# A greedy issue planner replaced by a fixed issue table, with MLP1 sums regrouped and the modulation rows sent through DRAM

## Chip, cores and metric

The kernel runs on one core of a Trainium2 chip. The metric is the device time of one execution in microseconds (us). The kernel before has a median of 216.2 us over 5 runs (215.92 to 216.38).

## Reference

One adaLN block with S = 2048 tokens and D = 512 channels, all bfloat16. `c` gives six modulation rows; a local dilated attention (window 8, step 2, 32 heads of 16) and a token-mixing MLP (2048 to 1792 to 2048, over tokens, not channels) follow.

```python
mod = (silu(c) @ w_mod).reshape(1, 6, 1, -1)        # sa, ca, ga, sb, cb, gb
h = layernorm(x) * (1 + ca) + sa
x = x + ga * attention(h, wqkv, wo)                 # k, v of positions s, s-2, ..., s-14
h = layernorm(x) * (1 + cb) + sb
hn = layernorm(h)                                   # the MLP's own norm
u = gelu(einsum('bsd,sf->bdf', hn, w1) + b1)        # sum over tokens s
y = einsum('bdf,fs->bds', u, w2) + b2
x = x + gb * y.transpose(0, 2, 1)
```

MLP1 sums over tokens, so no unit of it is complete before the last token tile has been through attention.

## The kernel before

**Tiles and chunks.** The tokens are 16 tiles of 128 (`st` = 0 to 15), taken through attention in five chunks of 2, 4, 4, 4 and 2 tiles (`SIZES`). MLP1's 1792 outputs are 14 units of 128 (`ft`), MLP2's tokens again 16 tiles.

**Steps and names.** Every piece of work is an `_Op` with a name, an engine (or a choice of two), what it reads and writes, and at times a buffer of a pool that it takes or frees. For a chunk `c` the steps are: `ln1s` (DVE statistics of x), `rstd1`/`nb1` (ACT and DVE, a tile's scale and shift), `n1` (the norm itself, on ACT, DVE or POOL as the strings `NE` say), `tr` and `hT` (transposes on PE and their copies; chunks 2 to 4 use DMA transposes `xt`), `wsc` (scaling of the qkv weights by 1+ca), `qkv` and `ev` (projection and copy out of PSUM), `vd` (16 DMAs a chunk that lay out shifted v), `qk` (DVE products q*k, 128x4096), `red` (PE sums of them over 16 channels), `max`, `sub`, `exp`, `esum`, `rcp`, `smB` (softmax), `a2` (weights spread to partitions), `pv` (DVE products, 128x4096) and `pvacc` (PE sums), `oev`, `wo` (output projection, residual), `x1` (copy to x), `ln2s` or `ln2q`/`ln2m` (second norm's statistics, on DVE or on ACT), `n2`, `aff` (times 1+cb, plus sb, on DVE), `ln3s`, `rstd3`, `h3` (the MLP's norm). `red`, `pvacc`, `a2` use 32-column tiles of the PE array (four matmuls side by side); all other matmuls use the whole array.

**MLP.** MLP1 is done in three levels over token tiles 0-5, 6-9 and 10-15 (`BOUNDS=(6, 10)`) for all 14 units. After level 0 the sums are parked in `gT` as bfloat16 (`park0`); level 1 begins with a matmul that puts them back into PSUM (`inj1`, `INJ=(1,)`) and parks again (`park1`); level 2 gets them added by DVE (`padd2`), then `gelu` on ACT. MLP2 is one group of 14 matmuls a tile (`mlp2`), then two DVE operations (`fin`) and a store.

**Modulation rows.** `build_mod_rows` forms ga, sb, 1+cb and gb as rows spread over all 128 partitions: `sc_rep` (silu(c) repeated over 128 columns) is the stationary operand, four matmuls of 512 columns a row, and ACT copies each row out of PSUM. `woq_s` multiplies the output weights by ga.

**Order.** `G.schedule()` simulates the engines at build time with a duration for each op, and at each step issues the op that can start first, with ties inside a window of 0.02 us (`WIN`) broken by the ranks `RANK`; `BIAS` shifts work between ACT and DVE. Each engine then runs its list in that order and waits in order. All compute instructions are recorded through one helper, so the profile shows them as line 238; tiles tell them apart. All DMAs but one are issued by SP; each waits for the one eight places before it.

**Warm-up.** 36 small matmuls (`warm`) and 42 planned ones (`filler`) run on PE before its first real work.

Of the kernel before, what the change touches and what calls it, by code (L numbers as in the profile page):

```python
# [8 lines left out]
ALU = mybir.AluOpType  # L9
# [14 lines left out]
class _Op:  # L24
    __slots__ = ("idx", "alts", "eng", "dur", "lat", "fn", "name", "deps", "succ", "start", "end", "bytes_", "pk", "bias",
                 "alloc", "frees", "behind", "locks", "desc")

    def __init__(self, idx, alts, lat, name, bytes_, pk):
        self.idx, self.alts, self.lat, self.name, self.bytes_, self.pk = idx, alts, lat, name, bytes_, pk
        self.eng, self.dur, self.fn = alts[0]  # L30
        self.deps, self.succ = set(), []
        self.start = self.end = None
# [9 lines left out]
class _Graph:  # L42
    XLAT = 0.05
    OVERLAP = {"dve": 0.08, "act": 0.1}
    PE_DRAIN = 0.17
    LANES = 8
    RING = 132
    PWAIT = 3.0
    WIN = 0.25

    def __init__(self, pools):
        self.pools = pools
        self.ops = []
        self.last_writer = {}
        self.readers = {}
        self.pk = 0.0
# [4 lines left out]
    def add_any(self, alts, reads=(), writes=(), name="", lat=0.0, after=(), bytes_=0, pk=None, bias=0.0, alloc=None,  # L61
                frees=None, behind=None, locks=False, desc=0):
        op = _Op(len(self.ops), list(alts), lat, name, bytes_, self.pk if pk is None else pk)
        op.bias, op.alloc, op.frees, op.behind = bias, alloc, frees, behind
        op.locks, op.desc = locks, desc
# [27 lines left out]
    def filler(self, t, n, k):  # L93
        f = _Op(-1, [("pe", n * 0.06, lambda: self.fill_fn(k, n))], 0.0, "filler", 0, 0.0)
        f.start, f.end = t, t + n * 0.06
        f.alloc = f.frees = f.behind = None
        f.locks, f.desc = False, 0
        return f

    def schedule(self):  # L100
        ops = self.ops
        for o in ops:
            for d in o.deps:
                ops[d].succ.append(o.idx)
        eng_free = {}
        dmaq = []
        locked = []

        def pool_end(r, d):
            t = r  # L110
            for a, b in locked:
                if b <= t:
                    continue
                if a > t:
                    if a - t >= d:
                        return t + d
                    d -= a - t
                t = b
            return t + d + (self.PWAIT if len(locked) > 4 else 0.0)
        ndeps = {o.idx: len(o.deps) for o in ops}  # L120
        avail = set(o.idx for o in ops if not o.deps)
        free = {k: {i: 0.0 for i in range(n)} for k, n in self.pools.items()}
        order = []

        def pick(slot):
            f = free[slot.pool]
            if slot.size == 1:
                return min(((f[k], (k ^ 1) in f, k) for k in f), default=None)
            return min(((max(f[k], f[k + 1]), k) for k in f if k % 2 == 0 and k + 1 in f), default=None)

        dep_ready = {}

        def ready_time(o, e):
            r = dep_ready.get((o.idx, e))
            if r is None:
                r = 0.0
                for d in o.deps:
                    od = ops[d]
                    if od is o.behind or od.eng == e == "pe":
                        t = od.start + od.dur  # L140
                    else:
                        t = od.end + self.XLAT
                    if t > r:
                        r = t
                dep_ready[o.idx, e] = r
            if o.alloc is not None and o.alloc.i is None:
                r = max(r, pick(o.alloc)[0] + self.XLAT)
            if o.bytes_:
                if len(dmaq) >= self.LANES:
                    r = max(r, dmaq[-self.LANES][1])  # L150
                n = o.desc
                for tr1, _, k in reversed(dmaq):
                    n += k
                    if n > self.RING:
                        r = max(r, tr1)
                        break
            return r

        while avail:
            per_eng = {}  # L160
            for i in avail:
                o = ops[i]
                if o.alloc is not None and pick(o.alloc) is None:
                    continue
                fin = [(max(ready_time(o, e), eng_free.get(e, 0.0)) + d, e, d) for (e, d, _) in o.alts]
                best_fin = min(f_ + (o.bias if e == "dve" else 0.0) for f_, e, d in fin)
                for f_, e, d in fin:
                    if f_ + (o.bias if e == "dve" else 0.0) <= best_fin + 0.05:
                        per_eng.setdefault(e, []).append((f_ - d, o, d))
            best = None  # L170
            for e, lst in per_eng.items():
                tmin = min(r for r, _, _ in lst)
                cands = [x for x in lst if x[0] <= tmin + self.WIN]
                r, o, d = min(cands, key=lambda x: (x[1].pk, x[1].idx))
                key = (r, o.pk, o.idx)
                if best is None or key < best[0]:
                    best = (key, e, r, o, d)
            _, e, r, o, d = best
            for (ae, ad, afn) in o.alts:
                if ae == e:  # L180
                    o.eng, o.dur, o.fn = ae, ad, afn
            o.start = r
            if e == "pe" and 0.0 < eng_free.get(e, 0.0) < self.FILL and r - eng_free[e] > 0.45:
                t0_ = eng_free[e]
                n_ = int((r - t0_ - 0.25) / 0.06)
                k_ = min(((f, k) for k, f in free["ps"].items()), default=(1e9, None))
                if k_[0] + 0.2 < t0_:
                    order.append(self.filler(t0_, n_, k_[1]))
            if o.alloc is not None:
                o.alloc.i = pick(o.alloc)[-1]  # L190
                for k in range(o.alloc.i, o.alloc.i + o.alloc.size):
                    del free[o.alloc.pool][k]
                o.alloc.t = 0.0
            if o.bytes_:
                tr1 = max(dmaq[-1][0] if dmaq else 0.0, r + o.dur) + o.bytes_
                o.end = tr1 + o.lat
                dmaq.append((tr1, o.end, o.desc))
            elif e == "pool":
                o.end = pool_end(r, o.dur)
            else:  # L200
                o.end = r + o.dur + o.lat + (self.PE_DRAIN if e == "pe" else 0.0)
            if o.frees is not None:
                o.frees.left -= 1
                o.frees.t = max(getattr(o.frees, "t", 0.0), o.end)
                if o.frees.left == 0:
                    for k in range(o.frees.i, o.frees.i + o.frees.size):
                        free[o.frees.pool][k] = o.frees.t
            eng_free[e] = r + o.dur - min(self.OVERLAP.get(e, 0.0), o.dur / 2)
            if e == "pool":
                eng_free[e] = o.end  # L210
            elif e == "dve" and o.locks:
                locked.append((r, r + o.dur))
                del locked[:-40]
            avail.discard(o.idx)
            order.append(o)
            for s_ in o.succ:
                ndeps[s_] -= 1
                if ndeps[s_] == 0:
                    avail.add(s_)
        order.sort(key=lambda o: (o.start, o.idx))  # L220
        return order
# [61 lines left out]
def _t_mm(cols, n=1):  # L283
    return n * (cols / 2400.0 + 0.004)


RANK = {'st1': -161.55, 'ln1': -82.53, 'tr': -159.39, 'qk_w': 84.81, 'v_w': 105.19, 'vd': 487.97, 'qk': 123.18,
        'sm': -242.3, 'pv': 12.39, 'wo': 357.24, 'ln2': 86.75, 'aff': 148.57, 'ln3': 98.08, 'mod': 159.99,
        'mlp': 794.19, 'pre': 3041.84, 'last': 5069.91, 'wm1': -892.56, 'w1': -974.42, 'wm0': -831.47, 'w0': -807.94,
# [6 lines left out]
def kernel(  # L296
# [8 lines left out]
    B_w2: bass.AP,  # L305
    B_b2: bass.AP,
    c: bass.AP,
    w_mod: bass.AP,
    out: bass.AP,
    SIZES=(2, 4, 4, 4, 2),  # L310
    BOUNDS=(6, 10),
    NPRE=6,
    WIN=0.02,
    NBIG: int = 3,
    NVD: int = 5,
    NHT: int = 2,
    NB=2,
# [769 lines left out]
```

## Time and profile before

| what | value |
|---|---|
| profiled execution, its time / its span | 216.19 us / 214.5 us |
| PE busy | 201.1 us (94%) |
| DVE busy | 168.1 us (78%) |
| ACT / POOL busy | 123.8 us (58%) / 24.3 us (11%) |
| first DVE product of attention (`qk0_0`) starts | 20.16 us |
| last `h3` ends | 149.1 us |
| last matmul group ends | 210.3 us |
| stages: start, attention, MLP tail, end | 20.2, 129.0, 61.2, 4.2 us |

Times inside the run are counted from the span's start. PE's ends are modelled, so its busy share is not a measure of its peak. A busy DVE is taken as it stands.

### The profile page before, as it was taken

The page shows a single profiled execution, that of the slowest core. Times are in us where ns is not written, and L with a number is a line of the kernel's source. Part 1 is how long each engine was busy: PE and PEld are TensorE (multiplying, and loading weights), DVE is VectorE, ACT ScalarE, POOL GpSimd, SP SyncE. Part 2 cuts the span into 40 slices and gives each one's busy share as a digit, 9 for nine tenths or more (in the row PEclk, how much of TensorE's full clock was granted, in tenths as well). Part 3 has the DMA queues.
Part 4 walks back from the last instruction along what each step waited for, and adds up shares of the span by engine and source line. Part 5 has one row for each costly group of instructions (what it writes and reads, how often), then busy time and mean ns, then how long its engine had stood idle before and what let it go on. Part 6 is the DMA issues. An engine that isn't in the chain of part 4 may idle for free.

```text
span 214.5 us, 3880 instructions
## 1 busy us (share of the span) xinstructions
PE 201.1 (94%) x1453; PEld 99.6 (46%) x1475; DVE 168.1 (78%) x256; ACT 123.8 (58%) x270; POOL 24.3 (11%) x43
## 2 busy tenths in 40 slices
PE   7788999799999999999999999988999999999992
PEld 7678345335444447443443344333444444444451
DVE  3789999699999999999999789997854445544553
ACT  3559588658789989988857668886852000000000
POOL 6030709100000000000000034034000000000000
PEclk9969999999999999999999999999999999999999
DMA  5999984359999999999999886449869110111011
GB/s 164 356 351 340 215 211 100 80 123 162 147 130 133 133 137 308 148 144 154 230 256 169 226 215 171 134 91 323 209 175 254 50 44 30 53 49 49 24 49 50
DMA packets 54182, 34.24 MB, mean 160 GB/s; under 512 B 18452, under 2 KB 54164, under 8 KB 54164
## 3 DMA queue, kind: packets, MB, share of 16 engines
q1 hardware_dynamic: 54156, 34.00, 74.1%
q8 instruction: 11, 0.18, 0.4%
q14 instruction: 7, 0.06, 0.1%
q10 hardware_dynamic: 8, 0.00, 0.0%
HBM read 22.03 MB, written 2.10 MB: 112 GB/s over the span
## 4 chain that ended last, share of the span: by engine, by line
PE 68%; DVE 13%; DMA 7%; SPq 5%; issue 3%; ACT 1%; POOLq 1%; DVEq 0%
PE psS L238 64%; DMA gT<-in_w_mod_dram 5%; SPq L238 5%; DVE h L238 4%; DVE big L238 4%; PE psL L238 4%; DVE st L238 3%; DMA hT<-h 2%; POOLq L1082 1%; DVE mv L238 1%; DVE xx L238 1%; ACT lv L238 0%; ACT o_sb L238 0%; ACT k_f L238 0%; ACT gT L238 0%
## 5 line engine op out<-in xcount | busy, mean ns | idle before, releaser
L238 PE MATMUL psS<-h,wst 128*128 128x512 bf16 x216 | 50.9, 379 | 1.7 <-POOL h L238 1.2
L238 PE MATMUL psS<-hT,w_qkv 128*128 128x512 bf16 (+1 forms) x234 | 46.5, 342 | 1.4 <-DMA hT<-h 1.1
L238 PEld LDWEIGHTS <-wst 128*128 128x128 bf16 x324 | 30.3, 99 | 35.4 <-issue 4.1
L238 PEld LDWEIGHTS <-w_qkv 128*128 128x128 bf16 x282 | 29.5, 113 | 23.6 <-issue 6.4
L238 DVE TENSOR_TENSOR big<-a2sb,vD 128x4096 bf16<-128x4096 bf16 (+1 forms) x20 | 37.0, 1864 | 2.5 <-DMA vD<-v_f 2.1
L238 DVE TENSOR_TENSOR big<-q_sb,k_f 128x4096 bf16<-128x4096 bf16 (+1 forms) x20 | 36.8, 1859 | 0.1
L238 DVE SCALAR_TENSOR_TENSOR h<-psS,bcol,gb_bc 128x512 f32<-128x512 f32 (+1 forms) x17 | 12.2, 720 | 24.6 <-PE psS L238 24.5
L238 ACT ACTIVATE gT<-psS 128x512 bf16<-128x512 f32 x28 | 15.9, 591 | 5.2 <-PE psS L238 5.2
L238 PE MATMUL psS<-gT,big 128*128 128x512 bf16 x83 | 18.2, 379 | 0.1
L238 DVE BATCH_NORM_STATS2 st<-xx 128x6 f32<-128x512 bf16 x21 | 14.2, 676 | 4.1 <-DMA xx<-in_A_x_dram 4.1
L238 PE MATMUL psS<-woq,o_sb 128*128 128x512 bf16 x61 | 16.2, 380 | 0.2
L238 PE MATMUL psS<-gT,wst 128*128 128x512 bf16 (+1 forms) x83 | 15.3, 343 | 0.1
L238 ACT ACTIVATE h<-xx,nb,rs 128x512 bf16<-128x512 bf16 x17 | 13.3, 810 | 2.7 <-DVE nb L238 2.7
L238 PEld LDWEIGHTS <-big 128*128 128x128 bf16 x116 | 9.2, 97 | 11.8 <-DMA big<-in_w_mod_dram 1.9
L238 PEld LDWEIGHTS <-ident 128*128 128x128 bf16 (+1 forms) x146 | 11.2, 110 | 6.8 <-issue 1.7
L238 POOL TENSOR_SCALAR h<-xx,mv,rs 128x512 bf16<-128x512 bf16 x2 | 4.3, 2136 | 87.7 <-DVE xx L238 87.2
L238 ACT ACTIVATE q_sb<-psS,qvb 128x512 bf16<-128x512 f32 (+1 forms) x20 | 11.7, 613 | 3.5 <-PE psS L238 3.4
L238 DVE TENSOR_TENSOR psS<-psS,gT 128x512 f32<-128x512 f32 x14 | 9.2, 695 | 4.6 <-PE psS L238 4.6
L238 POOL TENSOR_SCALAR h<-xx,rs,nb 128x512 bf16<-128x512 bf16 x7 | 10.4, 1489 | 15.6 <-DMA woq<-in_A_wo_dram 9.1
L238 ACT ACTIVATE v_f<-psS,qvb 128x512 bf16<-128x512 f32 (+1 forms) x20 | 11.5, 602 | 1.1 <-PE psS L238 0.7
L238 ACT ACTIVATE k_f<-psS 128x512 bf16<-128x512 f32 x16 | 9.6, 600 | 4.2 <-PE psS L238 3.9
L238 ACT ACTIVATE gT<-psS,bcol 128x512 bf16<-128x512 f32 x14 | 9.1, 687 | 4.7 <-DVE psS L238 4.7
(96 smaller groups left out, 232.8 us busy)
## 6 DMA issues: line engine op xcount, KB each, us to landing
vD<-v_f SPq DMA_DIRECT2D x48, 130.0 KB, 6.8
wst<-in_B_w_dram SPq DMA_DIRECT2D x6, 768.0 KB, 5.8
wst<-in_B_w_dram SPq DMA_DIRECT2D x4, 896.0 KB, 5.7
big<-in_B_w_dram SPq DMA_DIRECT2D x3, 896.0 KB, 6.4
vD<-v_f SPq DMA_DIRECT2D x32, 66.0 KB, 4.0
out_dram<-h SPq DMA_DIRECT2D x15, 128.0 KB, 1.7
xx<-in_A_x_dram SPq DMA_DIRECT2D x3, 512.0 KB, 10.2
gT<-in_w_mod_dram SPq DMA_DIRECT2D x3, 512.0 KB, 9.9
```

The lines of the kernel that those rows point to most:

```text
L238: r = fn(*a, **k)
L1082: with _tile.TileContext(nc) as tc:
```

## The change

The planner, its constants, `RANK` and `BIAS` go. `schedule()` now walks a table `ORDER` of 799 names; a suffix `:a` or `:d` picks ACT or DVE, `fill:k:n` puts n small matmuls there, and pool buffers are handed out by the oldest release. With the table come these changes of the work itself:

- The ACT table load is the first instruction of ACT, ahead of the load of c; the last chunk's x (`ld_x_4`, 256 KB) is the first DMA, and the DMA order of the start differs throughout.
- MLP1 is split by unit (`MIX`): units 0-6 keep levels 0-5, 6-9, 10-15; units 7-13 have two levels, 0-8 and 9-15, so they are parked once and never injected.
- The first MLP2 group is issued in three runs (units 0-8, 9-11, 12-13) with other groups between; the last tile's group is in pieces of 256, 128 and 128 columns instead of two of 256.
- The modulation rows are formed as columns (64 one-column matmuls), transposed by a matmul, stored to a DRAM scratch and read back spread over the partitions (`mcols`, `mrowt`, `mrows`, `st_row`, `ld_row`). The wide matmuls, `sc_rep` and the four row copies go.
- Norms are dealt out anew (`NE`): POOL has 18 instead of 11, DVE fewer. Tiles 10 to 12 get their second norm's statistics from ACT (`LN2D`, `X1D`). Five of the `wsc` go from DVE to ACT.
- 27 of the 36 warm-up matmuls stand at three later places (`warm3`, `warm1`, `warm0`).

On PE the 49 steps that use 32-column tiles form 39 separate islands among the full-array steps before and 22 after.

```diff
...
-        while avail:
...
+    def schedule(self):
+        by_name = {o.name: o for o in self.ops}
+        held = {p: [None] * n for p, n in self.pools.items()}
+        freed = {p: [-1] * n for p, n in self.pools.items()}
+        done, order = set(), []
+        for pos, token in enumerate(ORDER.split()):
+            name, *rest = token.split(":")
...
+            o = by_name.pop(name)
+            assert all(d in done for d in o.deps), name
+            for eng, dur, fn in o.alts:
+                if rest and eng[0] == rest[0]:
+                    o.eng, o.dur, o.fn = eng, dur, fn
+            if o.alloc is not None:
+                p = o.alloc.pool
+                o.alloc.i = min((freed[p][k], k) for k in range(self.pools[p]) if held[p][k] is None)[1]
+                held[p][o.alloc.i] = o.alloc
...
+            order.append(o)
+ORDER = """
+ld_x_4 halo0 act_table ident ld_x0 ld_x1 ld_c ld_x_1 consts ld_wmod1 ld_x_2 ld_wmod0 ln1s0 cps ld_wqkv0 warm2
+...
+pvacc0_3 vd1_00 modcol2 ev2_20:a qkv2_23 qkv3_10 ld_b2 a2ev1_1:a mcols0 xt14 pv1_2 mrowt0 qkv3_02 ev3_10:a
+vd1_01 mrows0:a ev2_21:a qkv3_00 st_row0 ev2_23:a pv1_1 vd1_03 red2_3 ev3_00:a pvacc1_2 vd2_00 oev0_2:a modcol3
+xt15 qk3_0 qkv3_11 vd1_02 ld_row0 qkv3_20 ev3_11:a vd2_10 qkv3_23 max2 vd2_20 qkv3_13 vd2_21 ev3_23:a pv1_3
+vd2_03 sub2 ev3_13:a qkv4_20 vd2_22 ev3_02:a vd2_23 exp2 qkv3_01 mcols1 vd2_30 woq_s pvacc1_1 ev4_20:a ev3_20:a
+...
+park1_0:a ld_w2_3 nb3_15 inj1_1 mlp1_1_1_6 h3_13 h3_11 h3_15 ln3s14 inj1_4 rstd3_10 rstd3_14 h3_10 mlp1_1_4_6
+park1_1:a h3_14 park1_2:d mlp1_1_8_9 ld_w1_2_0 park1_3:d park1_4:d mlp1_1_11_9 padd1_8 park1_5:a park1_6:a
+ld_w2_0 mlp1_1_9_9 mlp1_1_10_9 padd1_9 gelu9 mlp1_1_7_9 gelu8 mlp1_2_1_10 padd1_7 ld_w1_2_512 padd1_10
+...
+"""
-    BOUNDS=(6, 10),
+    MIX=((0, 7, (6, 10)), (7, 14, (9,))),
-    NE=('AADADAPPPAAPPPAP', 'AAAAADDADAPDPAAA', 'DADDDDDDAAAAPDPD'),
-    X1D=(10, 11, 15),
-    LN2D=(10, 11, 12, 14, 15),
+    NE=('PPAADPPPPPAAAPAA', 'APPPAAAADAPAAAPA', 'PPAPAADDPADAADDP'),
+    X1D=(14, 15),
+    LN2D=(14, 15),
...
-        add("dve", 0.4, lambda: nc.vector.tensor_copy(sc_rep[:], sc[:].unsqueeze(2).to_broadcast([P, KT, P])),
-            reads=["sc"], writes=["sc_rep"], name="sc_rep")
-        for r, t_, key in ((0, ga_bc, "ga_bc"), (2, ab_bc, "ab_bc"), (1, sb_bc, "sb_bc"), (3, gb_bc, "gb_bc")):
...
-                    nc.tensor.matmul(ps(s_), lhsT=sc_rep[:, kt, :], rhs=src[:, kt, :], start=(kt == 0),
-                                     stop=(kt == KT - 1))
...
+        for b_, (r0, nr) in enumerate(((0, 1), (1, 3))):
...
+                            nc.tensor.matmul(ps(s_)[:, r * KT + dt_:r * KT + dt_ + 1],
+                                             lhsT=w_[:, dt_ * P:(dt_ + 1) * P], rhs=sc[:, kt:kt + 1],
+                                             start=(kt == 0), stop=(kt == KT - 1))
...
+            dma(lambda scr=scr: scr.rearrange("r (t p) -> (r t) p", p=P), rows, 4 * nr * P * 2, [("mrows", b_)],
+                [("scr", b_)], f"st_row{b_}", lat=2.0)
+            dma(lambda r0=r0, nr=nr: rows_bc[:, r0:r0 + nr, :],
+                lambda r0=r0, nr=nr: bass.AP(scratch.tensor, scratch.offset + r0 * D, [[0, P], [D, nr], [1, D]]),
+                P * nr * D * 2, [("scr", b_)], ["ga_bc"] if b_ == 0 else ["sb_bc", "ab_bc", "gb_bc"], f"ld_row{b_}",
+                lat=2.0)
...
+            pieces = [(0, 256), (256, 128), (384, 128)] if st == NST - 1 else [(0, D)]
+            runs = [(0, 9), (9, 12), (12, NFT)] if st == 0 else [(0, NFT)]
```

## Prediction

> **What bounds the kernel now.** I read the page's shares first, then stages of the windows view, then the waits of the vector engine, then its timeline at the end of attention.
>
> The page's first part says that PE and DVE are both loaded:
>
> ```profile
> PE 201.1 (94%) x1453; PEld 99.6 (46%) x1475; DVE 168.1 (78%) x256; ACT 123.8 (58%) x270; POOL 24.3 (11%) x43
> ```
>
> The windows view, cut at the first attention product (20.16 us), the end of the last `h3` (149.14) and the last matmul group (210.30); columns are stage, length, then busy time (count) of PE, PEld, DVE, ACT, POOL, and PE clock, DMA share, GB/s:
>
> ```profile
> 0.00:20.16 20.16, 16.64 (x213) 15.23 (x214) 14.03 (x44) 11.63 (x26) 5.37 (x32) 0.92 0.95 302
> 20.16:149.14 128.98, 123.37 (x950) 55.37 (x966) 121.46 (x165) 102.34 (x232) 18.88 (x11) 1.00 0.92 173
> 149.14:210.30 61.16, 60.90 (x293) 28.97 (x296) 31.74 (x46) 9.80 (x15) 0.00 (x0) 1.00 0.35 93
> 210.30:214.50 4.20, 0.23 (x3) 0.00 (x0) 0.91 (x2) 0.00 (x0) 0.00 (x0) 0.90 0.12 34
> ```
>
> The reader is to see: in attention DVE works 121.46 of 128.98 us, so it idles 7.5 us; PE is close behind it; after 149.14 PE alone works, without a gap. The seam is the last `h3`, on which MLP1's last matmuls wait. DVE's waits up to there:
>
> ```profile
> DVE st L238 <- DMA xx<-in_A_x_dram: 4.1, 3, 3.0
> DVE big L238 <- DMA vD<-v_f: 2.1, 2, 1.9
> DVE m L238 <- PE psL L238: 1.7, 2, 1.5
> ```
>
> And the timelines at the seam (DVE, then PE):
>
> ```profile
> 147.08 0.69 DVE L238 BATCH_NORM_STATS2 st<-h 128x6 f32<-128x512 bf16 x1
> 147.81 0.18 DVE L238 BATCH_NORM_AGGREGATE mv<-st 128x2 f32<-128x6 f32 x1
> 148.59 0.55 DVE L238 TENSOR_SCALAR h<-h,mv,rs 128x512 bf16<-128x512 bf16 x1 [0.60 <-ACT rs L238]
> ```
> ```profile
> 149.04 13.11 PE L238 MATMUL psS<-h,wst 128*128 128x512 bf16 x59 [0.60 <-POOL h L238]
> ```
>
> So the time is: start of attention (20.16) + DVE work (121.46) + DVE idle (7.5) + PE tail (61.16) + end (4.20) = 214.5, and 1.7 us around the span.
>
> **What the Trainium skill says.** "TensorEngine Tiling (Array Packing)", Key Properties: changing the tiling mode drains PE. The trace agrees: in the PE timeline `wo0` with its 5 full matmuls and `red2_2` take 56.41 to 58.14 = 1.73 us, where 5 x 0.216 plus 8 x 512 columns four abreast (0.43) are 1.51; an island costs about 0.22 to 0.24. "GPSIMD Engine Reference", Specifications: POOL shares its SBUF interface with DVE. The trace agrees: a norm on POOL is 0.77 us at best, 2.1 beside DVE's norms and up to 3.86, and DVE's own scalings of 0.34 take 0.70 beside it. "DMA: Bandwidth & Descriptors", Anatomy: about 2.0 us fixed per DMA; here the shortest `vD` landing is 2.2 and the median 5.0, so queueing decides.
>
> **The change, part by part.** Durations are steps of the DVE timeline; neighbours overlap by 0.08 us (statistics pair 0.90 less 0.08 = 0.82, norm 0.33, copy from PSUM 0.61, product 2.20).
>
> *DVE between first product and last h3.* Taken out: five `ln1s` now stand ahead of the first product, 5 x 0.82 = 4.1; three `ln2s` (tiles 10-12) go to ACT, 2.5; eight norms go to POOL or ACT, 8 x 0.33 = 2.6, and `h3_15` 0.5; `x1_10`, `x1_11` 1.3; `biascols_cp` 0.1. Put in: `h3_10`, `h3_14` 0.7; `x1_14` 0.6; `a2ev4_0` 0.6; `mcols` 0.25; three `ln2m` 1.0; seven `nb` 0.5. Net -7.5: 121.5 becomes 114.0.
>
> *DVE before the first product.* 14.0 becomes 14.0 + 4.1 + 1.2 (`ev0_22`, two `hT`) - 1.4 (five `wsc`) - 0.35 (`sc_rep`) - 0.6 (`n1_2`) = 17.0. It idles 6.1 us there now, mostly for x. `ld_x_4` ahead of tiles 0 and 1 brings the first x later by 256 KB at some 350 GB/s, 0.7 us; with another 0.5 before chunk 1's x I take 4.2 idle and the first product at 21.2 (+1.0). The last qkv weights land after more bytes than before (4.2 MB instead of 3.4 in front), but DVE has statistics to do until then. Cover gone, each us there is one on the end. The ACT table load first delays c by 1.28 us: hidden, `silu_dve` now stands behind six statistics on DVE.
>
> *POOL.* 18 norms instead of 11, 7 more. Each can stretch a short DVE operation by up to 0.36 (`wsc`, above), or nothing beside a product. I take +1.0 in all (0 to 2.5). A norm delayed to 2 or 4 us can also hold up `aff`; that goes into the idle time.
>
> *DVE idle in attention.* The table starts `vd0` right behind `ev0_22`, at some 18 us instead of 25.1, so the 2.1 us of `vD` waits should go; the wait of 1.5 at `max4` and 0.6 at the last `h3` may. What is late next is unknown: 0 to 10 us. I take 4.5 (-3.0).
>
> *PE in attention.* Less: 17 islands x 0.24 = 4.1; seven injections x 0.216 = 1.5; the 16 wide row matmuls 3.45, against 64 one-column ones at 29 ns (16 of `modcols` take 0.46) = 1.9; 26 MLP1 matmuls moved behind the last `h3`, 5.6. More: 27 warm-ups x 0.055 = 1.5, one identity matmul 0.2. Sum -11: 123.4 becomes 112, under the 119.5 that DVE then needs. So PE's savings are worth nothing by themselves while DVE sets the seam; they would count if DVE were faster. The ten copies fewer of `park` are on ACT, which is not the bound.
>
> *PE tail.* After the last `h3` stand 91 MLP1 matmuls (49 for units 7-13, 42 for units 0-6) and 224 of MLP2, less 5 that need earlier tiles only: 310 x 0.216 = 67.0, plus 0.2 for the 128-column pieces, against 61.2: +6.0. `padd` and `gelu` run beside it as now (DVE 0.70 and ACT 0.69 a unit against 1.5 of PE). The W1 loads in the tail are covered: `ld_w1_2_0` (768 KB, median 5.8 us) by 35 matmuls, 7.6 us; `ld_w1_2_512` (576 KB, about 5.7) by 24, 5.2 us, so 0 to 1 us may show. The split first MLP2 group is worth nothing: no gap stands at that seam now. The smaller last piece ends DVE's last pair in about 0.55 instead of 0.9: -0.35.
>
> *Rows through DRAM.* Four DMAs more on SP, 0.6 us of issue each. `mcols0` to `woq_s` is now matmul, ACT copy, store, load: 6 to 15 us (two landings of 2.2 to 6.8). On DVE four products, `max2` and `mcols1` stand between, 4 x 2.2 + 1.3 = 10.1 us. Behind `woq_s` DVE's whole queue waits. 0 to 5 us, within the idle term.
>
> *Sum against the profiled execution:* +1.0 - 7.5 + 1.0 - 3.0 + 6.0 - 0.35 = -2.9; 216.19 becomes 213.3. The profiled execution stands at the median.
>
> **The rivals.**
> 1. *Covers hold.* The idle falls to 2 us and POOL costs nothing: 213.3 - 2.5 - 1.0 = 209.8. For it: PE, ACT and DMA all have less to do. Against it: every engine waits in order, and a fixed table cannot react.
> 2. *Slower: a new DVE stall.* The tail is 6 us longer for certain, and only an earlier seam pays for it. `woq_s` waits for ga through two DMAs behind the `vD` queue, or `pv1` stands ahead of its `vD` (issued up to 48 us or later, wanted from 50). Each us counts in full; from an idle of 7.4 us on there is no gain. With 5 us at this place: 9.5 idle, 218.3. For it: `vD` lands in up to 10.3 us, and the DMA share is 1.1 to 1.2 there. Against it: `vd0` starts 7 us earlier.
> 3. *No change.* Idle stays at 7.5: earlier seam and longer tail cancel, 216.2. A table that merely repeats the plan is excluded by the 22 islands instead of 39.
>
> **Numbers.** Forecast (idle 3 to 6.5) 0.47, rival 1 0.27, rival 2 0.20, rival 3 0.06. Prediction 213.3 us. The range takes in rival 1 and the idle up to 9: 209.3 to 217.8. Chances, with 0.2% (0.43 us) as about what a measurement of this kernel can tell from no change: faster 0.75, same 0.06, slower 0.19.
>
> **What would show it.** First product near 21, DVE busy near 115 between it and the last `h3`, that `h3` near 141, PE gapless from there for 67 us, `red` and `pvacc` in pairs. Wrong if DVE's waits on `vD` or on ga's row grow past 5 us, if PE shows a half clock after 20 us, or if PE has gaps behind the seam.

## The result, and the profile after

The changed kernel takes 217.9 us (median of 27 runs, 214.9 to 221.0) where the kernel before takes 216.3 (47 runs, 215.3 to 217.0). The ratio is 1.0035, with a 95% interval of 1.0017 to 1.0053: **slightly slower**, and the interval leaves out 1. Ratios and intervals, here and below, are of the means of those runs alone that lie within 1.5% of their kernel's fastest (217.0 us for the changed kernel), so they are not the quotients of the medians. The forecast was 213.3. The profiled execution took 217.94 us, with a span of 216.2. The wide scatter is new: runs with a mean PE clock (the share of its full clock that PE was granted) of 0.994 or more have a median of 216.6, those under 0.98 one of 218.4. So medians are read here beside their intervals.

The page's shares, as shown of before:

```profile
PE 198.1 (92%) x1513; PEld 103.4 (48%) x1534; DVE 164.6 (76%) x258; ACT 118.0 (55%) x270; POOL 23.8 (11%) x49
```

The windows view, cut at the same four events (first product, last `h3`, end of the last matmul group); columns as before:

```profile
0.00:23.91 23.91, 17.56 (x195) 16.10 (x197) 16.31 (x51) 12.91 (x28) 10.42 (x38) 1.00 0.94 281
23.91:144.52 120.61, 112.68 (x983) 54.96 (x996) 113.82 (x156) 93.93 (x227) 13.36 (x11) 0.99 0.70 157
144.52:212.90 68.38, 67.90 (x337) 32.37 (x342) 33.85 (x53) 11.18 (x18) 0.00 (x0) 1.00 0.51 132
212.90:216.20 3.30, 0.00 (x0) 0.00 (x0) 0.61 (x2) 0.00 (x0) 0.00 (x0) 0.81 0.17 42
```

The work came off as counted: DVE has 113.8 us between first product and last `h3` (114.0 counted, 115.0 with POOL's interference). What is new is idle time. DVE idles 6.8 us there and 7.6 us ahead of it. DVE's waits up to the seam, and PE's largest in attention (columns: total, times, longest):

```profile
DVE st L131 <- DMA xx<-in_A_x_dram: 5.9, 3, 4.0
DVE big L131 <- DMA vD<-v_f: 3.8, 2, 3.4
```
```profile
PE psS L131 <- DMA hT<-h: 3.9, 2, 2.5
```

The first x comes at 4.0 us, chunk 1's x costs another 1.4. The 3.4 us are `pv1_2` at 57.9, for which the last quarter of its `vD` lands at 57.7; the 2.5 are `qkv3_10`, which waits for the DMA transpose of tile 13. Both loads stand far back in one queue: SP issues almost without a pause from 21.9 to 76 us, 0.61 a `vD` and 1.2 a transpose. Behind the pause before `qkv3_10` PE's granted clock is 0.5 for 3.41 us, from 57.9 on; a half clock after 20 us was one of the signs of being wrong that the prediction named. The page's clock in 40 slices:

```profile
PEclk9999999999889999999999999999999999999998
```

The seam (ACT, then PE):

```profile
143.98 1.55 ACT L131 ACTIVATE gT<-psS 128x512 bf16<-128x512 f32 x3
```
```profile
144.61 7.71 PE L131 MATMUL psS<-h,wst 128*128 128x512 bf16 x35 [0.19 <-ACT gT L131]
```

PE waits 0.19 us, and not for `h3` itself but for a PSUM buffer that ACT's `park` copies free; these stand in ACT's queue behind the last tiles' `rstd`, which need DVE's statistics. ACT works there without a gap from 142.3 us on and DVE's last statistics end at 143.51, so DVE, ACT and PE arrive at the seam nearly together.

### The profile page after: what moved, and what is told of

It is laid out like the page before. It is cut to its first block, busy times and chain, and to the rows that moved or that the text cites. A ratio compares the mean times of both kernels' runs of the same rounds, so it can differ in the third digit from the quotient of the medians.

```text
span 216.2 us, 4015 instructions
## 1 busy us (share of the span) xinstructions
PE 198.1 (92%) x1513; PEld 103.4 (48%) x1534; DVE 164.6 (76%) x258; ACT 118.0 (55%) x270; POOL 23.8 (11%) x49
## 4 chain that ended last, share of the span: by engine, by line
PE 54%; DVE 25%; SPq 6%; DMA 6%; issue 4%; ACT 2%; POOL 0%; DVEq 0%; POOLq 0%
PE psS L131 51%; DVE big L131 9%; SPq L131 6%; DVE h L131 6%; DVE st L131 6%; DMA hT<-h 3%; DMA xx<-in_A_x_dram 3%; PE psL L131 2%; DVE mv L131 2%; ACT h L131 1%; DVE m L131 1%; DVE nb L131 1%; DVE lsb L131 0%; ACT gT L131 0%; POOL h L131 0%
## 5 line engine op out<-in xcount | busy, mean ns | idle before, releaser
L131 PEld LDWEIGHTS <-wst 128*128 128x128 bf16 x354 | 31.0, 99 | 34.9 <-issue 3.5
L131 DVE SCALAR_TENSOR_TENSOR h<-psS,bcol,rows_bc 128x512 f32<-128x512 f32 (+2 forms) x18 | 12.4, 690 | 20.1 <-PE psS L131 18.3
L131 POOL TENSOR_SCALAR h<-xx,rs,nb 128x512 bf16<-128x512 bf16 x13 | 14.7, 1133 | 87.1 <-DVE nb L131 87.1
L131 PE MATMUL psS<-gT,big 128*128 128x512 bf16 x83 | 18.7, 379 | 0.1
L131 DVE TENSOR_TENSOR psS<-psS,gT 128x512 f32<-128x512 f32 x14 | 9.2, 696 | 10.2 <-PE psS L131 10.2
L131 DVE BATCH_NORM_STATS2 st<-xx 128x6 f32<-128x512 bf16 x18 | 12.1, 675 | 5.9 <-DMA xx<-in_A_x_dram 5.9
L131 PE MATMUL psS<-gT,wst 128*128 128x512 bf16 (+2 forms) x95 | 15.3, 316 | 0.1
L131 DVE TENSOR_TENSOR h<-h,xx 128x512 bf16<-128x512 f32 (+2 forms) x18 | 11.4, 633 | 4.2 <-DMA out_dram<-h 3.6
L131 ACT ACTIVATE h<-xx,nb,rs 128x512 bf16<-128x512 bf16 x17 | 13.3, 805 | 1.1 <-DVE nb L131 1.1
L131 ACT ACTIVATE lv<-mv,epscol 128x1 f32<-128x1 f32 (+2 forms) x25 | 7.3, 294 | 12.0 <-DVE mv L131 11.4
L131 PEld LDWEIGHTS <-ident 128*128 128x128 bf16 x141 | 11.5, 116 | 4.0 <-issue 0.4
L131 DVE TENSOR_TENSOR h<-h,rows_bc 128x512 bf16<-128x512 bf16 (+2 forms) x20 | 12.0, 603 | 0.5
```

Source lines behind the costliest of these rows:

```text
L131: r = fn(*a, **k)
```

## The experiments

All times of the text count from the profile's zero; the expectations count from the first busy instruction, 0.3 us later. One place is a good anchor. In every profile of the table below that is read, and in e9's, the stretch from `a2_3_1` (chunk 3, 98.1 us in the changed kernel) to the end of the last store's issue is 115.8 us, to within 0.02: 115.82 in the changed kernel, 115.82 in e1, 115.80 in e4, 115.81 in e6, e9, e11, e14 and e15. So what moves a time in these is decided before `a2_3_1`. But its start is that of one execution. The changed kernel, e6, e8 and e9 have the same table up to there and show it at 98.1, 97.3, 96.2 and 97.9 us: a profile's difference of under 2 us says nothing by itself. The profiled execution of e17 ran at a mean clock of 0.66 and is not read.

| kernel | first product | `a2_3_1` | median us (runs) | ratio to before, 95% |
|---|---|---|---|---|
| changed | 23.9 | 98.1 | 217.9 (27) | 1.0017 to 1.0053 |
| e1, x_4 late | 23.6 | 96.5 | 216.5 (14) | 0.9982 to 1.0022 |
| e4, SP reordered | 25.2 | 97.0 | 216.9 (22) | 1.0013 to 1.0047 |
| e5, fillers | 24.9 | 97.5 | 218.5 (6) | 1.0081 to 1.0152 |
| e6, no split | 24.5 | 97.3 | 217.3 (22) | 1.0018 to 1.0062 |
| e7b, start and SP | 22.2 | 97.0 | 216.5 (14) | 0.9965 to 1.0021 |
| e14, start alone | 23.0 | 96.7 | 215.5 (22) | 0.9941 to 0.9978 |
| e16, SP alone | 25.8 | 99.2 | 218.4 (6) | 1.0063 to 1.0147 |
| e11, start and SP's pause | 21.4 | 94.7 | 214.2 (6) | 0.9883 to 0.9929 |
| e15, e11 and ga's row early | 21.8 | 94.2 | 215.1 (22) | 0.9932 to 0.9976 |
| e17, e15 and fillers | not read | not read | 214.6 (22) | 0.9909 to 0.9950 |

**e1: x_4 not first.**

```diff
-ld_x_4 halo0 act_table ident ld_x0 ...
+halo0 act_table ident ld_x0 ...
-... ld_x_3 fill:3:16
+... ld_x_3 ld_x_4 fill:3:16
-ln1s1 ln1s14 rstd1_0 ... ln1s15 ...
+... ln1s10 ev0_02:a qkv1_10 xt6 ln1s14 ln1s15 qk0_0
```

> The changed kernel with one load moved: x_4 is issued behind x_3 instead of first, and the statistics of tiles 14 and 15 stand right ahead of the first product. Theory 'start' (the early x_4 costs the seam): first x statistic at about 3.0 instead of 4.0 us, first product about 1.0 to 1.5 us earlier than 23.9, and the end 1 us earlier, ratio to the kernel before about 0.999. Rival 'filled anyway' (in the changed kernel DVE works on tile 14 while it waits for chunk 1, so it only swaps idle for work): first product within 0.4 us of 23.9 and no change of the time, ratio 1.003.

Measured: first statistic 2.9 us, first product 23.6, 1.4 us less at the median (the two intervals just overlap). Each theory has a half: the first product hardly moves, but the time falls. What the early x_4 does to the loads can be seen. Bytes moved in slices of 0.3 us from 0 to 12 us, of the changed kernel and then of e1:

```profile
GB/s 0 0 0 0 0 3 38 96 263 376 376 205 133 157 48 130 277 345 328 365 382 352 362 369 358 372 382 389 358 345 355 352 355 341 345 355 345 345 348 348
```
```profile
GB/s 0 0 0 0 0 3 219 225 106 283 99 27 205 239 372 369 355 358 382 393 382 386 365 372 345 345 352 348 348 352 341 348 352 341 358 338 352 355 338 352
```

With x_4 in front the full rate holds from 5.1 us on, in e1 from 4.2, and one of the 16 DMA engines lags: the first ends its part of chunk 1's x at 6.5 us, all but one by 7.6, the last at 8.5 (first 5.2, last 6.0 in e1). DVE begins on this x at 8.51, so it is the last engine that counts. The qkv weights of q are there at 14.5 instead of 12.1 and PE begins `qkv0_00` at 16.6 instead of 13.3. The 256 KB that I priced at 0.7 us cost 2.4 to 3.3 at these places. DVE does not turn this into an earlier product by itself: six statistics stand ahead of `qk0_0`, and it now waits 1.5 us for x_3. Where the 1.4 us of the median come from is not shown: e1's `a2_3_1` at 96.5 lies among the four that the changed kernel's own table gave.

**e4: SP's queue.**

```diff
-... ld_wmod4 hT1_3:a ...
+... ld_wmod4 ld_wmod3 ld_wo1 ld_b2 hT1_3:a ...
-xt13 qkv2_21 smB1 ev2_03:a vd1_21
+vd1_21 xt13 qkv2_21 smB1 ev2_03:a
```

> The changed kernel with SP's queue reordered: the loads of modulation block 3, wo's last quarter and b2 go into SP's pause ahead of the first vD (18 to 21.6 us), and the last vD quarter of pv1_2 goes ahead of the transpose of tile 13. Nothing else moves. Theory 'queue' (DVE's 3.4 us wait before pv1_2 and PE's 2.5 us wait before qkv3_10 are SP's issue time): both waits fall to 0.5 to 1.5 us, the last h3 comes 2 to 3 us earlier (141.5 to 142.5 instead of 144.5), ratio to the kernel before 0.990 to 0.994. Rival 'PE next' (PE's own queue from 56 to 84 us is as late as DVE): DVE's wait before pv1_2 goes but comes back at later copies and products, gain under 1 us, ratio 0.999 to 1.003.

Measured: `pv1_2` waits 0.2 us, PE's wait for tile 13's transpose is 1.5 us, and the last `h3` comes 118.2 us behind the first product instead of 120.6. But the first product is at 25.2, since PE ran at half clock from 10 to 20 us in this execution and DVE waited 1.8 us for `ev0_22`, its copy of v out of PSUM. The queue theory is right on the waits; at the median (-1.0 us) less than half of the gain arrives, and the ratio lies where the rival put it.

**e5: fillers in PE's pauses.**

```diff
-qkv2_11 ... qkv3_10
+fill:5:20 qkv2_11 ... fill:0:45 qkv3_10
```

> The changed kernel with 65 more dummy matmuls of 128 columns on PE: 20 ahead of qkv2_11 (where PE paused 1.5 us) and 45 ahead of qkv3_10 (where it paused 3.0 us). No result depends on them. Theory 'clock' (the pause before qkv3_10 is followed by 3.4 us at half clock, and this is what scatters the runs of the changed kernel between a mean clock of 0.96 and 1.0): every run shows a mean clock of 0.99 to 1.0, the half-clock window at 58 to 61 us is gone, and the median falls by 1 to 2 us to about 216.3, ratio 0.996 to 1.000. Rival 'not the pause' (the windows come from elsewhere): clocks scatter as before and the median stays at 217.5 to 218, ratio 1.002 to 1.006.

Measured: mean clocks still scatter from 0.967 to 0.999, and the six runs are not faster than the changed kernel's (217.4 to 220.2). "TensorE: Matmul & The Clock Gate", Part 1, of the Trainium skill says that a window of idle, some 3.4 us on a free-running count, halves the clock. The trace agrees on the length, since the half-clock stretch in the changed kernel is 3.41 us, but the pause ahead of it was only 2.5. With the fillers that stretch is gone, but the time stays: this profile has another, from 8.7 to 18.9 us, with a wait of 1.3 us for `ev0_22`. So the pause before `qkv3_10` is a sign of a late transpose, and filling it does not make the runs fast.

**e6: the first MLP2 group whole.**

```diff
-runs = [(0, 9), (9, 12), (12, NFT)] if st == 0 else [(0, NFT)]
+runs = [(0, NFT)]
-mlp2_0_0 ld_w2_11 ... gelu12 gelu13 mlp2_0_0b mlp2_4_0 ... mlp2_0_0c
+ld_w2_11 ... gelu12 gelu13 mlp2_0_0 mlp2_4_0 ...
```

> The changed kernel with the first MLP2 group in one piece again (14 matmuls behind the last gelu, instead of 9, 3 and 2 with other groups between). My prediction gave the split nothing: then no change, ratio 1.003. Rival 'seam' (the last unit's addition and gelu, 0.70 + 0.69 us, stand uncovered on PE's path without it): 0.7 to 1.6 us slower, ratio 1.006 to 1.011, and a PE gap of that size between MLP1's last and MLP2's first matmul.

Measured: same time within the intervals, and 115.81 us from `a2_3_1` on, as with the split. The split is worth nothing here. Up to there e6 has the changed kernel's table and yet `pv1_2` waits 1.1 us and `qkv3_10` 0.4: these two waits differ by some 2 us between the two executions. e8 and e9 show 1.4 and 1.1 for `pv1_2`, so the 3.4 of the changed kernel's profile is the highest of four. Whether these waits or the half clock at the start make the scatter is not shown; e6's runs of a clock under 0.98 and those of 0.994 or more lie closer together (medians 217.9 and 217.5) than the changed kernel's.

**e8 and e9: DVE or PE at the seam?** e8 leaves out the third norm's statistics of two tiles, e9 the seven injections.

```diff
# e8
+SKIP3=(10, 11)     # h3_10 and h3_11 use tile 12's statistics
-... ln3s10 ... ln3s11 ... rstd3_11 ... nb3_11 ... rstd3_10 ...
# e9
-inj1_0 ... inj1_6
+start=(s == s_lo)
```

> The changed kernel without the third norm's statistics of tiles 10 and 11 (1.64 us on DVE between 132 and 140 us, with their two rstd on ACT and one nb): the norms of these tiles use tile 12's statistics instead, so the output differs there. PE has the same work. Theory 'PE is the rail' (from 98 us on PE runs without a gap, so the end follows PE's sum and not the last h3): the last h3 comes about 1.5 us earlier, the time stays within 0.3 us of the changed kernel, ratio 1.002 to 1.005. Theory of the prediction (the last h3 is the seam, the end stands 67 to 68 us behind it): the end comes 1.3 to 1.8 us earlier, ratio 0.995 to 0.998.

> The changed kernel without the 7 injections of the first parked sum (7 matmuls of 512 columns on PE, 1.5 us, at 132 to 143 us, ahead of the last h3): the second sum leaves the first one out, so the output differs. DVE, ACT and POOL have the same work. Theory 'PE is the rail': the end comes 1.3 to 1.7 us earlier though the last h3 hardly moves (ratio about 0.996). Theory of the prediction (PE work ahead of the last h3 costs nothing while DVE sets the seam): the time stays as the changed kernel's, ratio 1.002 to 1.005, and a PE gap of about 1.5 us opens before the last h3.

The windows from `a2_3_1` to the last `h3`, of the changed kernel, e8 and e9 (length, then PE, PEld, DVE as above):

```profile
98.08:144.52 46.44, 44.53 (x335) 19.97 (x342) 44.84 (x91) 38.83 (x106) 4.09 (x5) 1.00 0.65 159
```
```profile
96.19:141.91 45.72, 44.23 (x339) 19.82 (x340) 43.36 (x86) 38.14 (x101) 4.09 (x5) 1.00 0.67 162
```
```profile
97.94:144.37 46.43, 43.49 (x334) 19.32 (x335) 44.82 (x91) 38.82 (x106) 4.09 (x5) 1.00 0.77 175
```

and e9's PE at the seam:

```profile
142.31 1.02 PE L131 MATMUL psS<-h,wst 128*128 128x512 bf16 x4 [0.42 <-ACT gT L131]
144.46 2.75 PE L131 MATMUL psS<-h,wst 128*128 128x512 bf16 x12 [1.13 <-ACT gT L131]
```

Counted from `a2_3_1`, e9's last `h3` and its end stay where they were to 0.01 us without 1.5 us of PE work; the freed time comes back as waits of 0.42 and 1.13. That is the prediction's reading: DVE sets the seam. But without 1.6 us of DVE work e8's last `h3` comes only 0.7 us earlier and its end 0.35, and PE has no gap left at the seam. DVE's other 0.9 us went into waits for ACT, 0.65 for a norm and 0.30 for an `rstd`. The changed kernel's group of `aff`, then e8's (last number: idle time ahead of it):

```profile
L131 DVE TENSOR_TENSOR h<-h,rows_bc 128x512 bf16<-128x512 bf16 (+2 forms) x20 | 12.0, 603 | 0.5
L131 DVE TENSOR_TENSOR h<-h,rows_bc 128x512 bf16<-128x512 bf16 (+2 forms) x20 | 12.0, 604 | 1.1 <-ACT h L131 0.7
```

So with DVE's work cut ACT holds the last `h3` after 0.7 us and PE the end after 0.35, and DVE alone is worth no more. My theory of a PE rail falls; that DVE alone sets the seam holds for a third of a microsecond. No run took work off ACT alone. The medians (216.8 and 216.6) lie below the changed kernel's, but carry the scatter from before `a2_3_1`.

**e10: the kernel before without its 14 injections.**

```diff
-add("pe", _t_mm(512), lambda ...: nc.tensor.matmul(ps(s_), lhsT=ident[:], rhs=gT[:, ft, :], ...
+add("pe", _t_mm(512), lambda: None, ...
```

> The kernel before without its 14 injections (14 matmuls of 512 columns on PE, 3.0 us, all ahead of its last h3); its planned order is the same, the output differs. If PE is the rail in the kernel before too (it was busy 123.4 of 129.0 us in attention, DVE 121.5): 2 to 3 us faster, ratio 0.986 to 0.991. If DVE sets its seam, as the prediction took it: under 0.6 us (the one PE wait at the seam), ratio 0.997 to 1.000.

Measured: 215.6 us, ratio 0.9949 to 0.9977. Of 3.0 us of PE work 0.8 arrives, a little more than the 0.6 that the prediction's reading allowed: PE did not set that seam either, but stood close behind. In the kernel before PE waited there 0.60 us for POOL's last norm, as the prediction's own line shows, and not for DVE's.

**e7b, e14, e16 and e11: which moves bring it back?**

```diff
# e14: the start
-ld_x_4 halo0 ...
+... ld_wqkv1 ld_x_4 n1_0 ln1s5 ... ld_x_3 ...
+... ln1s14 ln1s15 ln1s12 ...             # ahead of tile 12's
+qk0_0 ... qk0_3 ... ln1s11 ln1s10 rstd1_3 qkv1_23 qk1_0 nb1_3
# e16: SP alone
-vd0_03 ... ld_wmod3 ... ld_wo1 red1_0 ... vd1_30
+vd0_03 ... red1_0 ... ld_wmod3 ld_wo1 vd1_30
# e11: both.  e7b: e14, with ld_wmod3 behind vd1_21 and ld_wo1 behind vd1_32
```

> The changed kernel with four moves in its table: x_4 is issued just ahead of x_3 instead of first, the statistics of tiles 14 and 15 stand ahead of tile 12's, those of tiles 10 and 11 behind the first four products, and the loads of modulation block 3 and wo's last quarter go behind the last vD quarter of pv1_2. Theory 'start and SP queue' (PE's rail starts 2.5 us earlier once x_4 is out of the way, and PE need not wait for the first products): first product at about 20 us, a2_3_1 (from where PE runs on without a gap) at 95.0 to 96.0 instead of 97.8, ratio 0.992 to 0.997, below the kernel before. Rival 'DVE and SP give it back' (DVE's sum up to chunk 1's products and SP's issue rate set that place): ratio 0.999 to 1.002, as with x_4 moved alone.

> As the last table with moved loads, but the loads of modulation block 3 and wo's last quarter go into SP's own pause right ahead of the first vD of chunk 1 (33.9 to 35.7 us) instead of among chunk 1's vD, where DVE lost 2.1 us before pv1_1 and 0.7 before woq_s. Theory 'start and SP queue': both waits go, a2_3_1 starts at 94 to 95 instead of 96.7 (97.8 in the changed kernel), the end follows 115.8 us behind it, ratio to the kernel before 0.989 to 0.995. Rival 'another wait' (PE, or the next vD, is as late): a2_3_1 stays at 96 to 96.7, ratio 0.998 to 1.001.

> The changed kernel with the start's moves alone: x_4 just ahead of x_3, tiles 14 and 15's statistics ahead of tile 12's, those of tiles 10 and 11 behind the first four products. SP's later queue is the changed kernel's. If the start alone brings it: first product at 21 to 22, a2_3_1 at 94 to 95, ratio 0.990 to 0.994. If both are needed (SP's issue of chunk 1's vD sets pv1_2): first product as early, but DVE waits 1 to 2 us before pv1_2 and a2_3_1 starts at 95.5 to 96.3, ratio 0.996 to 1.001.

> The changed kernel with one move: the loads of modulation block 3 and wo's last quarter right ahead of the first vD of chunk 1. If SP's queue alone brings it: DVE's wait before pv1_2 under 1 us, a2_3_1 at 95 to 96, ratio 0.993 to 0.998. If both are needed (there is no pause of SP at that place as long as the start is late, so nothing is gained): a2_3_1 at 96.5 to 97.8, ratio 1.001 to 1.005.

In e7b `pv1_2` starts at 54.0, 3.8 us earlier than in the changed kernel, but its `pv1_1` then waits 2.1 us: the two loads moved now stand among chunk 1's `vD`, and `a2_3_1` gains 1.1 only.

```profile
DVE big L131 <- DMA vD<-v_f: 2.4, 2, 2.1
```

In e11 they go where SP has nothing to issue, and the windows are:

```profile
0.00:21.44 21.44, 16.29 (x195) 14.28 (x197) 15.11 (x47) 12.67 (x28) 10.36 (x38) 0.92 0.97 292
21.44:141.11 119.67, 111.72 (x983) 54.93 (x996) 115.31 (x160) 94.04 (x227) 11.35 (x11) 1.00 0.77 162
141.11:209.70 68.59, 67.90 (x337) 32.34 (x342) 34.06 (x53) 11.17 (x18) 0.00 (x0) 1.00 0.50 131
```

These lie close to the forecast's terms: first product 21.4 (21.2 forecast), DVE 115.3 (115.0) with 4.4 us idle (4.5), last `h3` 141.1 (140.7). In part that is luck: the statistics of two tiles (1.6 us) moved from ahead of the first product to behind it. Without that move DVE's work there would be some 113.7, and the first product up to 1.6 later. e11 takes 214.2 us, 0.9906 (0.9883 to 0.9929) of the kernel before, and beats both. The start alone (e14) brings 2.4 of the 3.7 us at the median. What SP's two loads add to it is less sure: e11 has six runs, and e15 (below), with one load more moved, is only 0.4 us under e14 in 22 runs each, with intervals that overlap. SP alone (e16) brings nothing: its start is the late one (first `vD` issued at 23.8, in e11 at 19.4), and SP has no pause ahead of chunk 1's first `vD`, where the two loads now stand. In its profile PE had half its clock from 15.1 to 21.9 us and DVE waited 2.7 us for `ev0_22`; whether that makes its median higher is open.

**e15 and e17: two remaining suspects.**

```diff
# e15 = e11 and
-xt15 qk3_0 qkv3_11 vd1_02 ld_row0
+ld_row0 xt15 qk3_0 qkv3_11 vd1_02
# e17 = e15 and
-fill:2:21 ... fill:5:6
+fill:2:36 ... fill:5:12
```

> The table of e11 with the broadcast load of ga's row issued ahead of the transpose of tile 15 (58.6 instead of 60.8 us). There DVE waited 1.5 us before woq_s for that row and PE 2.2 us behind it. Theory 'the DRAM route still stands in DVE's queue': the wait goes, a2_3_1 starts 1.0 to 1.5 us earlier than 94.4, ratio to the kernel before 0.983 to 0.987. Rival 'another wait takes its place' (pv1_0, or the vD behind the moved load): ratio 0.989 to 0.992, as e11.

> The table of e15 with 21 more dummy matmuls at the start (15 ahead of the first transposes, 6 ahead of chunk 1's), where PE pauses 1.2 and 0.4 us. In e11 PE's clock was halved from 12.7 to 16.1 us, and DVE waited 1.9 us before ev0_22. Theory 'the pauses halve the clock and this delays DVE': no half clock before 200 us, ev0_22's wait under 0.8, 0.8 to 1.3 us faster than e15. Rival 'the clock at the start is hidden or not set by these pauses': same time as e15 within 0.4 us.

In e11 one wait of those that the prediction feared is left, that for ga's row:

```profile
DVE woq L131 <- DMA rows_bc<-scratch: 1.5, 1, 1.5
```

In e15 it is gone, and two others come: PE 1.2 us for a DMA transpose, DVE 0.8 before `pv1_0`. `a2_3_1` gains 0.5 us, the medians (on different chips) gain nothing. So the rival's mechanism holds, though the ratio is above the 0.989 to 0.992 that it gave. e17's 0.5 us against e15 lies within the intervals and goes with no change of the clocks (10 of 22 runs at 0.994 or more, 13 of 22 in e15): the fillers do not hold the clock. The profiles lean to a cost of the half clock at the start. In the three without one there (changed, e1, e6) DVE waits 0.6 to 0.7 us for `ev0_22`; in e4, e5, e7b, e8, e9, e11, e14, e15 and e16, with 3.4 to 10.2 us of it, 0.8 to 3.1. DVE's wait in e1, then in e14:

```profile
DVE v_f L131 <- PE psS L131: 0.6, 1, 0.6
DVE v_f L131 <- PE psS L131: 3.1, 1, 3.1
```

No run changes the clock alone, so this stays a correlation.

**e12 and e13: parts of the change alone, with the old planner.**

```diff
# e12
-BOUNDS=(6, 10),
+MIX=((0, 7, (6, 10)), (7, 14, (9,))),
# e13: the new build_mod_rows() in the kernel before
```

> The kernel before, its planner and all its constants, with the new MLP1 sweeps alone (units 0 to 6 parked twice, units 7 to 13 once, at tile 9). The planned order is the same up to the end of chunk 2's copies. It takes 7 injections (1.5 us of PE) and 7 copies of park (4.8 us of ACT) out ahead of the last h3 and puts some 25 MLP1 matmuls behind it. Theory 'DVE's seam' (the last h3 is set by DVE, so PE work moved behind it is paid in full and what it frees ahead of it is idle): last h3 within 1 us of 148.8, tail 5 to 6 us longer, ratio 1.018 to 1.028. Rival 'PE and DVE together' (PE is nearly as late there, so most of what is taken out ahead of the seam comes back): last h3 3 to 5 us earlier, ratio 0.995 to 1.010.

> The kernel before, its planner and constants, with the new modulation rows alone (64 one-column matmuls, a store and a broadcast load through DRAM instead of 16 wide matmuls and four wide copies). PE has 1.5 to 2 us less, SP four DMAs more (2.1 us of issue), DVE 0.4 us more copies and the sc_rep copy less, and woq_s comes later. Theory 'PE's savings don't count while DVE and SP set the pace': ratio 0.998 to 1.003. Rival 'PE counts': ratio 0.990 to 0.994. Rival 'DRAM route in the way' (woq_s waits for its row at the head of DVE's queue): 1 to 4 us slower, ratio 1.005 to 1.018.

e12 takes 228.1 us (ratio 1.0535 to 1.0573). Its windows (attention, then the tail to 222.0) and its clock in 40 slices:

```profile
20.25:152.63 132.38, 119.09 (x928) 53.63 (x942) 121.36 (x165) 98.64 (x227) 18.75 (x11) 0.98 0.91 174
152.63:222.00 69.37, 68.78 (x315) 31.91 (x321) 31.77 (x46) 9.97 (x15) 0.00 (x0) 0.96 0.27 71
```
```profile
PEclk9959999999999999999988999985999999999999
```

DVE's work is the old 121.4, but it idles 11.0 us instead of 7.5, the last `h3` is 3.5 us later and the tail longer: the mechanism expected, and worse in size. Two half-clock stretches of 3.4 and 6.8 us (near 117 and 151 us) are part of it, the second behind a pause of 4.3 us in which PE waits for POOL's norm: at half the clock they hold back at most 5.1 us of PE's work (my estimate, half their length). e13 takes 221.8 (1.0248 to 1.0289), 5.8 us more than before, and one of DVE's waits explains 3.5 of them:

```profile
DVE woq L238 <- DMA rows_bc<-scratch: 3.5, 1, 3.5
```

There `woq_s` stands early in the plan. Both parts cost more alone than the whole change does. What pays for them in the changed kernel must be among the rest, the order of the table and the new division of norms; these two were not run apart.

## Why the prediction was wrong, step by step

- **Work on DVE and POOL**: right. 113.8 us against 114.0 counted; of the 1.0 us set aside for POOL's interference nothing appeared (-1.2 in the sum).
- **First product, 21.2**: 23.9, **+2.7, the largest miss**. DVE's work ahead of it was near (16.3 for 17.0). The idle term is the step that failed, 7.6 us for 4.2. The 4.2 were 3.7 for the first x and 0.5 for the next; measured are 4.0, another 1.9 for x, 1.1 for two waits on PE that I put at nothing, and 0.6 in small pieces. I priced x_4 ahead of the others as its bytes over the rate; e1 shows that it delayed the following loads by 2.4 us and more. I also took a late qkv weight as hidden by DVE's statistics, without looking at PE, which starts 3.3 us later for it. x_4 is not all of it: with it moved back the first product comes only 0.3 us earlier (e1), and the 21.4 of e11 also takes the statistics of two tiles out from ahead of it.
- **DVE idle in attention, 4.5**: 6.8, **+2.3**. Right that the old `vD` waits of 2.1 would go with an earlier `vd0`. What would come in their place I left open and took at less than it was: `pv1` stood ahead of its `vD`, the place that rival 2 named, with 3.4 us in the profiled run and 1.1 to 1.4 in e6, e8 and e9. Its other place, ga's row, cost nothing in the changed kernel, since `pv1_2` was late already; it shows as 1.5 us in e11, once the first is gone.
- **Tail, 67.2**: 68.4, +1.2. The count was right (295 full matmuls and 14 worth of small ones, so 309). At the rate of before's own tail (60.90 us for 279 such matmuls, 0.218 each, where I took 0.216) they are 67.5 us; PE is busy for 67.9 and idle for 0.5.
- **End, 3.85**: 3.3, -0.55.
- Sum: -1.2 + 2.7 + 2.3 + 1.2 - 0.55 = +4.5, from 213.3 to the 217.9 of the profiled execution, with rounding.
- **Split for nothing, `padd`, `gelu` and the W1 loads covered**: right (e6).
- **PE's savings worth nothing while DVE sets the seam**: right in e9, but by a narrower margin than I took. I compared the sums over all of attention, 112 against 119.5, and read 7.5 us of slack. Of PE's idle 7.9 us 6.0 lie before 98 us; behind it the two are 0.35 us apart at the seam.
- **The likeliest case**: rival 2's mechanism came, in the profiled run at two thirds of its size and in others at a quarter, together with a cost that no rival had. The sign of the change is wrong. The range of 209.3 to 217.8 ends just under the 217.9 (and takes in the mean of 217.0), because it held the start fixed at 21.2 at both ends, though I had written myself that each us there is one on the end once its cover is gone.

## What to carry to other kernels

Price a load put ahead of others by when the last DMA engine finishes the loads behind it, not by its bytes (here 2.4 us and not 0.7). A fixed issue table is only as good as its queues' fronts: the same work took 217.9 us, or 214.2 (e11, six runs) to 215.1 (e15), by where nine or ten names stood. Before you move work off one engine, compare the engines stretch by stretch from the end backwards: slack summed over a whole stage may lie where it cannot be used.

## What was not expected of the hardware

- With a 256 KB load of later rows first, the last of the 16 DMA engines ended 2.0 to 2.7 us behind the first at chunk 1's x (changed, e4, e5, e6, e16); with that load behind the others the lag was 0.5 to 0.8 us (e1, e11, e14). In both the changed kernel and e1, single packets took 0.4 to 1.1 us between 2.9 and 5.4 us, where the median is 0.046. Why is open.
- The same table waited 3.4, 1.1, 1.4 and 1.1 us for the same `vD` in four executions (changed, e6, e8, e9). One profile shows one draw of such a wait.
- A pause of PE of 2.5 us was followed by 3.41 us at half clock in the changed kernel, one of 2.2 us by 3.41 in e7b, while pauses of 1.5 and 1.6 us before `qkv3_10` in e4 and e8 were not; in e16 such a stretch came behind pauses of 0.9 and 0.5 us. So the length of a pause alone does not tell.
